# A fused chunk attention and leaky-ReLU layer pair: first layer in seven products for 15 of 18 blocks, sums kept in PSUM, uniform blocks, a new written-out order

## The chip, the core and the metric

The kernel runs on one core of a Trainium2 chip. TensorE multiplies 128x128 stationary tiles with moving tiles and writes PSUM; VectorE and ScalarE work in SBUF and PSUM; GpSimd works in SBUF and issues the loads; SyncE issues transposing DMAs and the stores. The engines run side by side and meet by semaphores. The metric is the device time of one execution in microseconds.

## The reference

q, k and v have 8 batches, 8 heads, 576 rows and 64 columns. Each 64-row chunk attends to itself; the result, as 4608 tokens of 512 columns, goes through two layers with a leaky ReLU between them.

```
scores = scale * np.matmul(q_c, k_c.transpose(0, 1, 2, 4, 3))      # chunks of 64 rows
scores = scores - np.max(scores, axis=-1, keepdims=True)
attn = np.exp(scores)
attn = attn / (np.sum(attn, axis=-1, keepdims=True) + 1e-09)
out = np.matmul(attn, v_c)
x = out.transpose(0, 2, 1, 3).reshape(B * S, H * D)               # 4608 x 512
h = x @ w_in                                                      # w_in 512 x 2048
g = np.maximum(0.01 * h, h)
return (g @ w_out).astype(np.float32)                             # w_out 2048 x 512
```

## The kernel before

*Attention* goes by 36 units of 128 tokens (two chunks of all heads). A unit u is loaded by `load_qk` (`g`, L91); its q and k are transposed by TensorE (`tq`, `tk`, tiles qp and kp, L512 and L517) or by SyncE's DMA (`tdq`, `tdk`, tiles QT and KT, L564 and L558) and copied to QZ and KT (`q`, `k`, `cq`). Then come scores (`s`, tile Sp, L584), maximum and difference (`m`, `b`, L593 and L598), exponential (`x`, tile ex, L604), its sum, a small addition and reciprocal (`z`, L610 to L614), the scaling (`n`, tile en, L620, on GpSimd from unit 10), a transpose (`e` and `c`, or `d` by DMA, L643), the product with v (`v`, tile xp, L656) and the copy to xT (`a`, L677), a ring of 1536 tokens.

*The layers* go by 19 blocks: two of 128 tokens and 17 of 256. The first layer of blocks 0 to 8 is plain: `mm1` (`A`, `M`, tile hT, L319), then `act1` (L333). Blocks 9 to 18 take it in seven half-size products in place of eight (Strassen's scheme in Winograd's form): token sums xs of x (`xs`, L387, mostly on GpSimd), weight sums WS (L365), products 1 to 7 (`wide`, `V`, L416) for both halves s of the hidden columns. Products 1, 6, 7 and 4 accumulate in one PSUM bank, xbank; after 1, 6 and 7 ScalarE copies the bank to SBUF (`lx`, tile xkeep, L447); products 2, 5 and 3 go to banks of their own (xpr) and VectorE adds them to the copies (`la`, L453); the leaky step reads copies or bank (`lp`, L435, a few on VectorE, L431).

*The second layer* is in seven products for all blocks of 256 tokens: token sums SG (`sum`, L203), weight sums TW (L174), `product` (`R`, L227: prX accumulates products 1, 6, 7 and 4; prW, prZ and pr take the others), `combine` (`comb`, L260 to L281). The two 128-token blocks use `mm2` (`B`, tile oP, L462).

Matmuls on a constant tile (`i`, tile idle, L686) fill TensorE's queue at the start. The order of all work is one hand-written list, ORDER: each word issues one step on its engine, and engines run their instructions in that order. BANKS names the PSUM bank of tiles that share four banks; qp, kp, ox and Sp have one each.

Of the kernel before, what the change touches and what calls it, by code (L numbers as in the profile page):

```python
# [16 lines left out]
def kernel(  # L17
# [36 lines left out]

# [3 lines left out]


# [47 lines left out]
    def load_w_in(f0, f1):
        for m in range(2):
            nc.gpsimd.dma_start(
                out=w_inT[m * CH:(m + 1) * CH, :, f0:f1],  # L110
                in_=moe_w_in[m * d_model // 2:(m + 1) * d_model // 2, f0:f1].rearrange("(t d) f -> d t f", d=D),
            )
# [45 lines left out]
    banks = iter(BANKS)

    def mm():  # L160
        return "m" + next(banks)

    TW: dict[int, bass.AP] = {}
    SG: dict[tuple[int, int], bass.AP] = {}
    bank: dict[tuple[int, str], bass.AP] = {}
    kept: dict[tuple[int, str], bass.AP] = {}
    opened: set[tuple[int, str]] = set()

    def weight_sum(n):
        b11, b12 = w_outT[:, :HF, :HM], w_outT[:, :HF, HM:]  # L170
        b21, b22 = w_outT[:, HF:, :HM], w_outT[:, HF:, HM:]
        x, y = {1: (b12, b11), 2: (b22, TW.get(1)), 3: (b22, b12), 4: (b21, TW.get(2))}[n]
        TW[n] = sbp.tile([128, HF, HM], FP16, name=f"TW{n}")
        nc.vector.tensor_tensor(out=TW[n], in0=x, in1=y, op=ALU.subtract)  # L174

    def rows(j):

        nh = BLOCKS[j] // 2
        halves_of = slice(0, nh), slice(nh, 2 * nh)
        return halves_of[::-1] if j in EARLY else halves_of  # L180

    def token_sums(j, n):
        if (j, n) in SG:
            return
        if j in EARLY:
            for a, p in {
                1: [(a, 1) for a in range(4)], 2: [(0, 2), (1, 2)], 3: [(0, 1), (1, 1), (0, 2), (1, 2)], 4: [(2, 2), (3, 2)],
            }[n]:
                need("act", j, a, p)
        if n in (2, 4):  # L190
            token_sums(j, n // 2)
        nh = BLOCKS[j] // 2
        one, two = rows(j)
        a11, a12 = gT[j][:, :HF, one], gT[j][:, HF:, one]
        a21, a22 = gT[j][:, :HF, two], gT[j][:, HF:, two]
        SG[j, n] = sbp.tile([128, HF, nh], FP16, name="SG", tag="gS", bufs=4, padded_shape=[128, HF, 128])
        x, y, op = {
            1: (a21, a22, ALU.add),
            2: (SG.get((j, 1)), a11, ALU.subtract),
            3: (a11, a21, ALU.subtract),  # L200
            4: (a12, SG.get((j, 2)), ALU.subtract),
        }[n]
        (nc.gpsimd if (j, n) in SG_POOL else nc.vector).tensor_tensor(out=SG[j, n], in0=x, in1=y, op=op)  # L203

    def product(j, n, i):
        one, two = rows(j)
        g, w = gT[j], w_outT
        where, left, right = {
            1: ("X", g[:, :HF, one], w[:, :HF, :HM]),
            2: ("W", g[:, HF:, one], w[:, HF:, :HM]),  # L210
            3: ("Z", SG.get((j, 4)), w[:, HF:, HM:]),
            4: ("X", g[:, HF:, two], TW.get(4)),
            5: ("Z", SG.get((j, 1)), TW.get(1)),
            6: ("X", SG.get((j, 2)), TW.get(2)),
            7: ("X", SG.get((j, 3)), TW.get(3)),
        }[n]
        if where != "X" and j in ONE:
            where = n
        if (j, where) not in bank:
            tag = None if j in EARLY else {"X": "qp", "Z": None if j in ZMM else "kp"}.get(where)  # L220
            bank[j, where] = psp.tile([128, 2, HM], FP32, name=f"pr{where}", tag=tag or mm(), bufs=1)
        to = bank[j, where]
        if j == LAST and n == 4:
            last_product(left, right)
            return
        for f in range(HF):
            nc.tensor.matmul(  # L227
                out=to[:, i, :],
                lhsT=left[:, f, i * 128:(i + 1) * 128],
                rhs=right[:, f, :],  # L230
                start=(j, where) not in opened,
# [641 lines left out]
```

## Time and profile before

Three runs: 274.97, 274.99 and 275.19 us. The profiled execution's span is 273.3 us; its own time stands in no record beside that span.

| engine | busy us | share of the span |
|---|---|---|
| TensorE | 265.9 | 97% |
| VectorE | 219.9 | 80% |
| ScalarE | 208.8 | 76% |
| GpSimd | 165.3 | 60% |

Busy time is the time in which at least one instruction of an engine runs. Matmuls overlap, so the duration of one is longer than the step from one to the next. The stretches of the profile give busy time, instructions and clock between two points of time; the chain follows what released each step back from the last instruction.

### The profile page before, as it was taken

To read this page: it belongs to the slowest core of one execution; us is meant where nothing else is said; L and a number is where in the kernel's file an instruction comes from. 1 tells how busy PE (TensorE), PEld (TensorE's weight loads), DVE (VectorE), ACT (ScalarE), POOL (GpSimd) and SP (SyncE) were. 2 spreads that over 40 slices of the span, in tenths; PEclk is the share of its full clock that TensorE was granted. 3 is DMA by queue.
4 is the path that set the end of the run, shared out by engine and by line. 5 is a ranking of instruction groups with operands and counts; after the bars stand their busy time and mean duration, and the time that the engine had idled before them with its cause. 6 is when DMAs were issued, how large, how long until landed. Compare 5 with 4: busy or idle time off the path is not lost.

```text
span 273.3 us, 9009 instructions
## 1 busy us (share of the span) xinstructions
PE 265.9 (97%) x3705; PEld 242.4 (89%) x3705; DVE 219.9 (80%) x427; ACT 208.8 (76%) x410; POOL 165.3 (60%) x190
## 2 busy tenths in 40 slices
PE   7889999999999999999999999999999999999994
PEld 3579958999999899998989999999999998999994
DVE  7786869999997668798677987977899879488783
ACT  6667635665779688666999989899999998857560
POOL 8848546783175448649689799689895636012100
PEclk9999999999999999999999999999999999999999
DMA  9999999999999999999999999799999503131113
GB/s 147 155 188 191 206 178 156 176 117 130 210 138 169 171 140 119 195 219 168 164 189 153 203 160 124 139 134 180 95 147 158 134 2 101 22 98 40 41 41 115
DMA packets 159241, 38.34 MB, mean 140 GB/s; under 512 B 150240, under 2 KB 154720, under 8 KB 159200
## 3 DMA queue, kind: packets, MB, share of 16 engines
q0 software_dynamic: 111392, 18.10, 98.3%
q1 hardware_dynamic: 46768, 19.41, 38.7%
q8 instruction: 29, 0.48, 0.7%
q10 hardware_dynamic: 1040, 0.26, 0.4%
q14 instruction: 12, 0.10, 0.2%
HBM read 36.70 MB, written 9.44 MB: 169 GB/s over the span
## 4 chain that ended last, share of the span: by engine, by line
PE 86%; DVE 5%; ACT 3%; POOL 3%; issue 2%; POOLq 0%; DVEq 0%; ACTq 0%
PE hT L319 20%; PE prX L227 20%; PE xbank L416 11%; PE xpr L416 9%; PE prZ L227 6%; PE pr L227 6%; PE prW L227 3%; PE Sp L584 3%; PE xp L656 3%; PE oP L462 3%; ACT QZ L539 1%; ACT gT L435 1%; PE kp L512 1%; PE qp L512 1%; POOL SG L203 1%
## 5 line engine op out<-in xcount | busy, mean ns | idle before, releaser
L319 PE MATMUL hT<-xT,w_inT 128*128 128x128 f16 (+1 forms) x768 | 62.4, 237 | 0.0
L319 PEld LDWEIGHTS <-w_inT 128*128 128x128 f16 x768 | 53.6, 98 | 2.8
L227 PEld LDWEIGHTS <-SG 128*128 128x128 f16 x544 | 51.0, 98 | 5.4
L620 POOL TENSOR_TENSOR en<-ex,zi 128x512 f16<-128x512 f16 x26 | 28.2, 1085 | 40.1 <-DVE zi L614 19.8
L453 DVE TENSOR_TENSOR xkeep<-xpr,xkeep 128x512 f32<-128x512 f32 x60 | 39.6, 681 | 13.7 <-ACT xkeep L447 9.6
L333 ACT ACTIVATE gT<-hT 128x512 f16<-128x512 f32 x64 | 36.6, 595 | 9.0 <-PE hT L319 8.9
L227 PEld LDWEIGHTS <-gT 128*128 128x128 f16 x400 | 37.3, 98 | 4.3 <-ACT gT L435 0.4
L447 ACT ACTIVATE xkeep<-xbank 128x512 f32<-128x512 f32 x60 | 34.6, 593 | 7.4 <-PE xbank L416 7.0
L416 PEld LDWEIGHTS <-WS 128*128 128x128 f16 x640 | 38.0, 98 | 0.5
L91 POOL DMA_DIRECT2D q_in<-in_q_dram x39 | 33.4, 861 | 7.0 <-DMA w_outT<-in_moe_w_out_dram 3.0
L91 POOL DMA_DIRECT2D k_in<-in_k_dram x39 | 32.6, 838 | 7.8 <-DMA VB<-in_v_dram 3.3
L227 PE MATMUL prX<-TW,SG 128*128 128x256 f16 x272 | 35.3, 273 | 0.0
L435 ACT ACTIVATE gT<-xkeep 128x512 f16<-128x512 f32 x56 | 33.4, 631 | 2.1 <-DVE xkeep L453 1.8
L260 ACT ACTIVATE keep<-prX 128x256 f32<-128x256 f32 x51 | 19.6, 384 | 16.9 <-PE prX L227 16.5
L416 PEld LDWEIGHTS <-w_inT 128*128 128x128 f16 x480 | 29.0, 98 | 0.9 <-issue 0.4
L203 DVE TENSOR_TENSOR SG<-gT 128x1024 f16<-128x1024 f16 x34 | 25.2, 740 | 4.7 <-ACT gT L333 2.9
L610 DVE TENSOR_REDUCE z<-ex 128x8 f32<-128x512 f16 x36 | 24.4, 679 | 4.9 <-ACT ex L604 4.7
L593 DVE TENSOR_REDUCE mx<-Sp 128x8 f32<-128x512 f32 x36 | 24.4, 677 | 4.5 <-PE Sp L584 4.5
L573 ACT ACTIVATE QZ<-QT 64x512 f16<-64x512 f16 x44 | 27.3, 627 | 0.9 <-PE Sp L584 0.3
L677 ACT ACTIVATE xT<-xp 128x512 f16<-128x512 f32 x36 | 21.5, 596 | 6.0 <-PE xp L656 5.8
L387 POOL TENSOR_TENSOR xs<-xT 128x256 f16<-128x256 f16 x18 | 12.5, 701 | 20.7 <-ACT xT L677 20.7
L98 POOL DMA_DIRECT2D VB<-in_v_dram x24 | 23.4, 987 | 0.0
(92 smaller groups left out, 486.0 us busy)
## 6 DMA issues: line engine op xcount, KB each, us to landing
out_dram<-osb SPq DMA_DIRECT2D x35, 256.0 KB, 4.1
q_in<-in_q_dram POOLq DMA_DIRECT2D x31, 128.0 KB, 5.9
k_in<-in_k_dram POOLq DMA_DIRECT2D x31, 128.0 KB, 6.7
VB<-in_v_dram POOLq DMA_DIRECT2D x8, 288.0 KB, 9.1
VB<-in_v_dram POOLq DMA_DIRECT2D x16, 144.0 KB, 5.3
w_inT<-in_moe_w_in_dram POOLq DMA_DIRECT2D x8, 256.0 KB, 7.2
w_outT<-in_moe_w_out_dram POOLq DMA_DIRECT2D x4, 512.0 KB, 11.6
q_in<-in_q_dram POOLq DMA_DIRECT2D x8, 64.0 KB, 6.3
```

What stands on the lines that cost most here:

```text
L91: nc.gpsimd.dma_start(out=to, in_=rows)
L203: (nc.gpsimd if (j, n) in SG_POOL else nc.vector).tensor_tensor(out=SG[j, n], in0=x, in1=y, op=op)
L227: nc.tensor.matmul(out=to[:, i, :], lhsT=left[:, f, i * 128:(i + 1) * 128], rhs=right[:, f, :], start=(j, where) not in opened, stop=(f == ...
L319: nc.tensor.matmul(out=hT[:, i, :], lhsT=w_inT[:, t, fc * 128:(fc + 1) * 128], rhs=xT[:, t, r0:r0 + tb], start=(t == 0), stop=(t == NT - 1),)
L333: nc.scalar.activation(out=gT[j][:, nf * a:nf * a + nf, c0:c0 + tb], in_=HT.pop((j, a, p)), func=AFT.Prelu, bias=0.0, scale=1.0, alpha=0.01,)
L416: nc.tensor.matmul(out=to[:, i, :], lhsT=left[:, t, i * 128:(i + 1) * 128], rhs=right[:, t], start=(n in (1, 2, 5) and t == 0 and i == 0), ...
L435: nc.scalar.activation(out=gT[j][:, f0:f0 + 4, hi * 128:hi * 128 + 128], in_=of, func=AFT.Prelu, bias=0.0, scale=1.0, alpha=0.01)
L447: nc.scalar.activation(out=XK[j, s, n], in_=XB[j, s], func=AFT.Copy, bias=0.0, scale=1.0)
L453: nc.vector.tensor_tensor(out=to, in0=of, in1=to, op=ALU.add)
L573: nc.scalar.activation(out=to, in_=QT[u][part], func=AFT.Copy, bias=0.0, scale=1.0)
L593: nc.vector.tensor_reduce(out=MX[u], in_=SP[u], axis=AXL.X, op=ALU.max)
L620: (nc.gpsimd if u >= UP else nc.vector).tensor_tensor(out=E[u], in0=ex, in1=ZI.pop(u).unsqueeze(2).to_broadcast((128, 8, CH)), op=ALU.mult)
```

## The change

Blocks are now 18 of 256 tokens. Blocks 0, 1 and 2 keep the plain first layer, in parts of 128 tokens; blocks 3 to 17 take it in seven products. All 18 take the second layer in seven. The wide sums are now made so: after product 1, the bank is copied to another bank (`ls`, tile seed) and product 2 accumulates on it; product 5 starts a bank xz, which is copied to SBUF (`lf`, tile x5); after product 6 VectorE adds xbank and x5 into xz (`la` with 3), where product 3 accumulates; after product 7 it adds xbank and x5 into x5 (`la` with 7). The leaky step reads seed, xz, xbank and x5. A mark ' on a word moves a step to the other engine: copies from ScalarE to VectorE, token sums and `n` from VectorE to GpSimd, z's small addition from VectorE to ScalarE. BANKS names the bank among eight for every PSUM tile and the slot of every SBUF tile. ORDER and the order of the loads are new throughout.

```diff
-    BLOCKS = 2 * [128] + 17 * [256]
-    EARLY = (2, 3, 4)
+    BLOCKS = 18 * [256]
+    LATE = (0, 1, 2)
+    FIVE = (0, 1, 2, 15, 16, 17)
+    HELD = 3
...
-        XK[j, s, n] = sbp.tile([128, 4, 128], FP32, name="xkeep", tag="xkeep", bufs=6)
-        nc.scalar.activation(out=XK[j, s, n], in_=XB[j, s], func=AFT.Copy, bias=0.0, scale=1.0)
...
-        nc.vector.tensor_tensor(out=to, in0=of, in1=to, op=ALU.add)
...
+    def wide_seed(j, s, other=0):
+        XW[j, s] = ps([128, 4, 128], "seed")
+        copy(other, XW[j, s], XB[j, s])
+
+    def wide_five(j, s, other=0):
+        X5[j, s] = sb([128, 4, 128], FP32, "x5", "xkeep", 6)
+        copy(other, X5[j, s], XZ[j, s])
+
+    def wide_add(j, s, n):
+        to = XZ[j, s] if n == 3 else X5[j, s]
+        nc.vector.tensor_tensor(out=to, in0=XB[j, s], in1=X5[j, s], op=ALU.add)
...
-        (nc.gpsimd if (j, n) in SG_POOL else nc.vector).tensor_tensor(out=SG[j, n], in0=x, in1=y, op=op)
+        (nc.gpsimd if other else nc.vector).tensor_tensor(out=SG[j, n], in0=x, in1=y, op=op)
...
-        "i33 y4 y2 I y0 y6 y1 tq0 q0.0 q0.1 w3 tk0 i5 k0 i6 s0 tq1 i4 m0 b0 q1.1.1 i13 tk1 q1.0.1 x0 k1 tq2 i8 s1 tk2 "
-        "z0 m1 b1 k2.1 n0 i6 q2.0.1 q2.1.1 x1 i9 i7 i13 e0 c0.1 z1 s2 tk3 v0 tq3 m2 n1 b2 a0 e1 c1 i7 v1 A0.0 x2 a1 "
+        "g2 y0 y1 i5.1 i73.0 y2 g1 I y4 If y3' i15.3 tq2 tk0 k0 tq0 tk2 q0.0 q0.1 tq1 s0 tk1 q1.1 q2.0' k2' q1.0 q2.1' s2 "
+        "m0 g3 tq3 k1 s1 tk3 b0 x0 q3.1 i25.4 m2 m1 b1 k3 q3.0 x1 s3 g6 tq6 b2 z0.0 z0.1 z1.0 x2 z0.2 q6.1 z2.0 tk6 i8.7 "
+        "g5 tk5 m3 L0 n0 z1.1 z1.2 tq5 q5.0 k6 i52.6 e0 i27.5 g4 z2.1' q6.0 tq4 y6' Q3 b3 x3 n1 e1 z2.2 z3.0 q5.1 n2 tk4 "
+        "z3.1 c0 z3.2 e2 Q1 k5 s5 v0 g8 q4.0' g7 Q0 c1 n3 e3 v1 k4 s6 a0 c2' v2 q4.1' s4 c3 v3 M0.3.1 a1' i2.2 m4 a2 "
```

On ScalarE, halfway through the program, copies of xbank to xkeep (L447) stood between the second layer's copies (keep, L260) and leaky steps (L435):

```order
L447 ACTIVATE xkeep<-xbank 128x512
L260 ACTIVATE keep<-prX 128x256
L447 ACTIVATE xkeep<-xbank 128x512
L435 ACTIVATE gT<-xkeep 128x4x128
L447 ACTIVATE xkeep<-xbank 128x512
L573 ACTIVATE QZ_67<-QT 64x8x64
```

The same place of the changed program, where a copy goes to a PSUM bank (seed, L200) or from xz to x:

```order
L384 ACTIVATE gT<-x_2868 128x4x128
L200 ACTIVATE seed<-xbank 128x512
L200 ACTIVATE keep<-prX 128x256
L384 ACTIVATE gT<-seed 128x4x128 x2
L200 ACTIVATE x_3238<-xz 128x512
L384 ACTIVATE gT<-xz 128x4x128
```

Leaky steps now read PSUM banks for three of four quarters, and of three copies two are left.

On VectorE, about half of its rows in, the sums of first-layer products (L453), combined outputs (osb, L281), token sums (SG, L203) and attention stood so:

```order
L203 TENSOR_TENSOR SG<-gT 128x1024
L453 TENSOR_TENSOR xkeep<-xpr,xkeep 128x512 x2
L281 TENSOR_TENSOR osb_3071<-prZ,keep 128x256
L593 TENSOR_REDUCE mx<-Sp 128x8
L453 TENSOR_TENSOR xkeep<-xpr,xkeep 128x512 x2
L281 TENSOR_TENSOR osb_2909<-prZ,keep 128x256
L203 TENSOR_TENSOR SG<-gT 128x1024
L203 TENSOR_TENSOR SG<-SG,gT 128x1024
L598 TENSOR_TENSOR Sp<-Sp,mx 128x512
```

In the changed program, at the same count of rows:

```order
L198 COPY QZ_66<-QT 64x8x64
L288 TENSOR_TENSOR Sp<-Sp,mx 128x512
L461 TENSOR_TENSOR x_2578<-xbank,x_2578 128x512
L502 TENSOR_TENSOR SG<-SG,gT 128x1024
L284 TENSOR_REDUCE mx<-Sp 128x8
L563 TENSOR_TENSOR ob<-prZ,keep 128x256
L502 TENSOR_TENSOR SG<-gT 128x1024
L198 COPY keep<-prX 128x256
L461 TENSOR_TENSOR xz<-xbank,x_2773 128x512
```

The copy of prX (keep) came from ScalarE, a sum is written to the bank xz, and the copy into QZ has come too; the small addition to z has gone to ScalarE in places.

On GpSimd, behind the first loads, all instructions were loads (q_in, k_in, VB of v, w_outT):

```order
L91 DMA k_in<-in_k_dram 128x8x64
L121 DMA w_outT<-in_moe_w_out_dram 128x4x512 x4
L91 DMA q_in<-in_q_dram 128x8x64
L91 DMA k_in<-in_k_dram 128x8x64
L98 DMA VB_64<-in_v_dram 64x36x64 x2
```

There the scaling of attention (en, L309) and a token sum (SG, L502) now stand between loads:

```order
L146 DMA w_outT<-in_moe_w_out_dram 128x4x512
L309 TENSOR_TENSOR en<-ex,z_829 128x512
L146 DMA w_outT<-in_moe_w_out_dram 128x4x512
L502 TENSOR_TENSOR SG<-gT 128x1024
L117 DMA q_in<-in_q_dram 128x8x64
```

Loads behind the token sum are issued after it.

More of the change, by code (lines that the diff above doesn't have):

```diff
@@ L158 @@
[L158 to L183, printed above, removed]
-            return
[L185 to L231, printed above, removed]
-                stop=(f == HF - 1),
-                skip_group_check=True,
-            )
-            opened.add((j, where))
@@ L497, with idle, copy @@
+    def idle(n, _=0):
+        t = ps([128, 512], "idle")
+        for i in range(0, n, 3):
+            c = 128 * min(3, n - i)
+            nc.tensor.matmul(out=t[:, :c], lhsT=warm[:, :128], rhs=warm[:, :c], start=True, stop=True)
+    def copy(other, to, of):
+        if other:
+            nc.vector.tensor_copy(out=to, in_=of)
+        else:
+            nc.scalar.activation(out=to, in_=of, func=AFT.Copy, bias=0.0, scale=1.0)
     QP: dict[int, bass.AP] = {}
@@ L651, in stage_v @@
[L651 to L652 removed]
+        XP[u] = ps([128, NT, 2, CH], "xp")
         for e in range(2):
@@ L666, in stage_v @@
-            if c == NCH - 1:
-                made.add(("batch", b))
-        XP[u] = xp
-    def load_v_piece(b, i):
-        made.add(("vl", b, i))
-        load_v_heads(b, i % 2, i // 2 * H // 4, i // 2 * H // 4 + H // 4)
-    def stage_a(u):
-        xp = XP.pop(u)
-        at = u * G % RING
-        nc.scalar.activation(out=xT[:, :, at:at + G], in_=xp, func=AFT.Copy, bias=0.0, scale=1.0)
-        assert state["tokens"] == u * G
-        state["tokens"] = (u + 1) * G
-    def idle(n):
-        t = psp.tile([128, 512], FP32, name="idle", tag=mm(), bufs=1)
-        for i in range(0, n, 3):
-            c = 128 * min(3, n - i)
-            nc.tensor.matmul(out=t[:, :c], lhsT=warm[:, :128], rhs=warm[:, :c], start=True, stop=True)
@@ L735, with stage_a, hidden, part_of @@
-    ORDER = (
[84 rows of a table removed]
+    def stage_a(u, other=0):
+        at = u * G % RING
+        copy(other, xT[:, :, at:at + G], XP[u])
+        groups.add(u)
+    gT: dict[int, bass.AP] = {}
+    HT: dict[tuple[int, int, int], bass.AP] = {}
+    def hidden(j):
+        if j not in gT:
+            gT[j] = sb([128, NFC, BLOCKS[j]], FP16, "gT", "gT", 3, padded_shape=[128, NFC, NB])
+        return gT[j]
+    def part_of(j, p):
+        return (128, (p - 1) * 128) if p else (BLOCKS[j], 0)
+    def mm1(j, a, p=0):
+        tb, c0 = part_of(j, p)
+        rows_ready(START[j] + c0, START[j] + c0 + tb)
+        r0 = (START[j] + c0) % RING
+        nf = 512 // tb
+        hT = ps([128, nf, tb], "hT")
+        for i in range(nf):
+            fc = nf * a + i
+            for t in range(NT):
+                nc.tensor.matmul(
+                    out=hT[:, i, :],
+                    lhsT=w_inT[:, t, fc * 128:(fc + 1) * 128],
+                    rhs=xT[:, t, r0:r0 + tb],
+                    start=(i == 0 and t == 0),
+                    stop=(t == NT - 1),
+                    skip_group_check=True,
+                )
+        HT[j, a, p] = hT
@@ new lines, in last_product @@
+    def last_product(left, right):
+        r0 = START[LAST] + halves_of(LAST)[1].start
+        for c in range(0, HM, HM // 2):
+            cut = slice(c, c + HM // 2)
+            of = ps([128, HM // 2], "prL")
+            for f in range(HF):
+                nc.tensor.matmul(out=of, lhsT=left[:, f, :], rhs=right[:, f, cut], start=(f == 0), stop=(f == HF - 1))
+            to = ob[LAST, 1][:, cut]
+            nc.vector.tensor_tensor(out=to, in0=of, in1=kept[LAST, 7][:, cut], op=ALU.add)
+            nc.sync.dma_start(out=out[r0:r0 + 128, cut], in_=to)
```

682 lines of the change are left out of this document (289 added, 393 removed), and 169 rows, old and new, of the table ORDER.

## The prediction, made before the changed kernel ran

> **What bounds the kernel now.** I read the page's shares first, then busy time by stretch.
>
> ```profile
> span 273.3 us, 9009 instructions
> PE 265.9 (97%) x3705; PEld 242.4 (89%) x3705; DVE 219.9 (80%) x427; ACT 208.8 (76%) x410; POOL 165.3 (60%) x190
> ...
> 0.00:20.00 20.00, 16.41 (x237) 11.16 (x238) 15.66 (x33) 12.96 (x19) 14.26 (x25) 1.00 1.62 162
> 20.00:60.00 40.00, 40.00 (x603) 35.48 (x601) 32.80 (x62) 24.93 (x50) 28.17 (x34) 1.00 1.98 172
> 60.00:100.00 40.00, 40.00 (x525) 37.06 (x524) 32.52 (x69) 28.66 (x57) 19.26 (x20) 1.00 1.89 161
> 140.00:180.00 40.00, 39.82 (x594) 37.74 (x592) 33.96 (x66) 37.10 (x75) 34.47 (x40) 1.00 1.53 152
> 180.00:220.00 40.00, 39.98 (x597) 37.85 (x595) 32.86 (x61) 38.09 (x79) 30.60 (x32) 1.00 1.27 140
> ```
>
> The columns of the stretches are PE, weight loads, VectorE, ScalarE, GpSimd, then granted clock (1.00 throughout) and DMA. From 20 us on TensorE misses 0.2 us in 160. The kernel is bound by the length of TensorE's queue. ScalarE at 95% (38.09 of 40) and VectorE at 85% (33.96) did not yet stall it. Next, the start in order of time (start us, us, engine, line, tiles, count, idle time before it and its releaser):
>
> ```profile
> 1.33 3.50 PE L686 MATMUL idle<-warm 128*128 128x384 f16 x11 [1.33 <-DVE zeros L137]
> 7.43 0.41 PE L584 MATMUL Sp<-KT,QZ 128*128 128x64 f16 x8 [0.72 <-DVE QZ L541]
> 11.59 2.07 PE L686 MATMUL idle<-warm 128*128 128x384 f16 x13
> 14.01 0.40 PE L628 MATMUL tpe<-ident,en 128*128 128x128 f16 x4 [0.35 <-DVE en L620]
> 17.44 1.95 PE L319 MATMUL hT<-xT,w_inT 128*128 128x128 f16 x32
> ```
>
> Until 17.44 us the queue holds attention of the first units, filler ("idle" products on a constant tile), and waits for VectorE and ScalarE. The first eleven fillers take 3.50 us, 0.32 each; thirteen later ones take 2.07, 0.16 each. So filler is real queue time: an idle product too many costs 0.16 us.
>
> A matmul's own duration is no price, since they overlap; the chain that ended last gives prices, for runs of equal matmuls:
>
> ```profile
> 22.68 3.58 PE hT L319 x64
> 34.53 1.73 PE oP L462 x8
> 124.39 1.75 PE hT L319 x16
> 154.79 0.89 PE xbank L416 x16
> 155.68 0.87 PE prX L227 x8
> 268.87 0.91 PE prL L244 x16
> ```
>
> That is 0.0556 us for 128 columns (0.89/16, 3.58/64), 0.109 for 256 (0.87/8, 1.75/16) and 0.216 for 512 (1.73/8). The chain's last matmul ends at 269.8; the end behind it (VectorE's sum, the last stores) is 3.5 us of the 273.3. The median of the runs, 274.99, stands 1.7 us above this span, and I carry the 1.7 over.
>
> **The change, part by part: TensorE.** *First layer.* Before: 512 plain matmuls of 128 columns, 256 of 256, 1120 of the seven-product kind: 28.5 + 27.9 + 62.3 = 118.7 us. Now 384 plain ones and 15 blocks of 112, 1680: 2064 x 0.0556 = 114.8. Gain **3.9 us**.
>
> *Second layer.* Before: 944 of 256 columns and 32 of 512 (the two 128-row blocks): 102.9 + 6.9. Now 1000 of 256: 109.0. The 16 halves of the last product stay. Gain **0.8**.
>
> *Transposes.* Units 11 to 13 go through SyncE's DMA in place of TensorE: 24 fewer, **1.3**. They add six transposing DMAs; SyncE's queue, 90 instructions long, has no compute behind it.
>
> *Filler.* 41 idle products become 72; those of 384 columns grow from 34 to 66. 32 x 0.16 = **5.1 us more**. Useful work shrinks by 6.0, the queue by only **0.9**. So the result hangs on waits.
>
> **Waits at the start.** In the table of stretches' manner, TensorE is idle 3.6 us of the first 20 (16.41 busy; 1.3 before anything is there); counting from matmul start to matmul start and taking off the prices above, the waits there cost 4.5 us beside the 1.3 and the slow first fillers, since each wait also drains the pipeline. Now seven units' scores stand before the first layer's first matmul. Walking the order: tq2, tk0, tq0, tk2, tq1 run from 7.9 to 10.3 us; s0 needs both halves of QZ, two ScalarE copies behind k0, about 10.9: a wait of 0.55. s1 and s3 wait 0.5 each for k1 and q3.0, v3 0.2 for c3. That is 1.8, and about 1.2 for changes of kind where a weight load isn't hidden: 3.0 against 4.5. Gain **1.5**. Bounds: all 4.5 saved, or, if the walk errs by a step or two of 0.7 us on ScalarE, 1 lost. The first plain matmul then starts near 24.5 us, not 17.4. Its weights (the last quarter of w_in, now loaded behind six units and a batch of v) come by GpSimd's queue; two issues in order of time, and the page's row on issues with its median from issue to landing:
>
> ```profile
> 16.31 0.62 POOL L109 DMA_DIRECT2D w_inT<-in_moe_w_in_dram  x1 [0.61 <-DMA w_inT<-in_moe_w_in_dram]
> 17.59 0.61 POOL L109 DMA_DIRECT2D w_inT<-in_moe_w_in_dram  x1 [0.65 <-DMA w_inT<-in_moe_w_in_dram]
> ...
> k_in<-in_k_dram POOLq DMA_DIRECT2D x31, 128.0 KB, 6.7
> ```
>
> Each half quarter (0.5 MB read) follows the last by 1.3 us; GpSimd waits for a landing before it issues another, so the loads run at the DMAs' pace. The first unit lands 6.7 us after its issue at 1.25, near 8; five more units of 0.5 MB, the batch of 1.2 MB and two half quarters at 1.3 us for 0.5 MB are 12.2 more: near 20, an estimate from these rows, and 22.5 if the units' shorter rows go at three quarters of that rate. Hidden, with 2 us of cover at the worse end. Were loads 3 us later than that, first layer and end would move by 1.
>
> **VectorE, ScalarE and GpSimd.** Prices of what moves, from the groups of instructions (count | busy us, mean ns of one | idle time before):
>
> ```profile
> L612 DVE TENSOR_TENSOR ze<-z,tiny 128x8 f32<-128x8 f32 x36 | 6.6, 182 | 1.2
> L453 DVE TENSOR_TENSOR xkeep<-xpr,xkeep 128x512 f32<-128x512 f32 x60 | 39.6, 681 | 13.7 <-ACT xkeep L447 9.6 <-PE xpr L416 3.9
> L203 DVE TENSOR_TENSOR SG<-gT 128x1024 f16<-128x1024 f16 x34 | 25.2, 740 | 4.7 <-ACT gT L333 2.9 <-ACT gT L435 1.8
> L281 DVE TENSOR_TENSOR osb<-prZ,keep 128x256 f32<-128x256 f32 x22 | 9.3, 421 | 4.6 <-PE prZ L227 3.1 <-ACT keep L260 1.2
> L541 DVE COPY QZ<-qp 64x512 f16<-64x512 f16 x19 | 7.9, 417 | 1.8 <-ACT QZ L539 1.5 <-PE qp L512 0.2
> L387 DVE TENSOR_TENSOR xs<-xT 128x256 f16<-128x256 f16 x2 | 0.6, 282 | 0.0
> L447 ACT ACTIVATE xkeep<-xbank 128x512 f32<-128x512 f32 x60 | 34.6, 593 | 7.4 <-PE xbank L416 7.0 <-DMA out_dram<-osb 0.2
> L203 POOL TENSOR_TENSOR SG<-gT,SG 128x1024 f16<-128x1024 f16 x8 | 17.4, 2173 | 9.3 <-DVE SG L203 4.0 <-ACT keep L260 2.7 <-ACT xkeep L447 2.6
> L620 POOL TENSOR_TENSOR en<-ex,zi 128x512 f16<-128x512 f16 x26 | 28.2, 1085 | 40.1 <-DVE zi L614 19.8 <-ACT xkeep L447 9.8 <-ACT gT L435 3.0
> ```
>
> A seven-product half now needs two copies and two sums of 512 columns, before three and three; with 30 halves for 20 the sums stay 60. VectorE loses 13 token sums (-9.6 us), 13 copies into QZ (-5.4) and 17 small sums of z (-3.1, at 0.182); it gets 17 copies of 256 columns (+7.1), 14 of 512 and 7 of xT (+14.3), 9 from QT (+3.8, at the nearest row; at least +1.8 by half of it), 17 token sums of x (+4.8), and leaky steps, en and the rest (+4). Sum: +16 of durations, +11 if each overlaps the next as L453 does (busy 39.6 for 60 x 681 = 40.9, and its follower starts earlier still): 219.9 becomes **231 to 236 us**. ScalarE loses 14 copies of 512 (-8.3), 13 of 256, 7 of xT: to below 200. GpSimd gets 17 token sums x 2.17 = +36.9: about 201. Neither is full. Copies from a bank to another bank (seed) aren't in the trace; nearest is L447, 0.593, and nothing says by which sign it differs: 0.4 to 0.8 on 30 ScalarE and VectorE copies, off the path unless those engines bind.
>
> VectorE is nearer to it: summed along the order by these prices (0.60 where rows follow each other), 178 us of its work stand before block 11's first second-layer product, R11.1, and 188 of TensorE's. It can't begin scores before s0, 11.2 us, with 4.6 done: 185 of 188. I take no stall beyond the 0.3 that the stretches show, since ScalarE at 95% cost no more.
>
> Sum: 274.99 - 0.9 (queue) - 1.5 (start) = **272.6 us**.
>
> **Rivals.** *VectorE loses turns to GpSimd (slower).* Two meetings in order of time, the group of GpSimd's xs, and token sums by tile (least/median/greatest ns):
>
> ```profile
> 76.52 1.32 POOL L620 TENSOR_TENSOR en<-ex,zi 128x512 f16<-128x512 f16 x1 [3.68 <-DVE zi L614]
> 76.86 1.53 DVE L203 TENSOR_TENSOR SG<-gT,SG 128x1024 f16<-128x1024 f16 x1
> 204.40 1.98 DVE L203 TENSOR_TENSOR SG<-gT 128x1024 f16<-128x1024 f16 x1
> 204.76 1.06 POOL L620 TENSOR_TENSOR en<-ex,zi 128x512 f16<-128x512 f16 x1
> ...
> L387 POOL TENSOR_TENSOR xs<-xT 128x256 f16<-128x256 f16 x18 | 12.5, 701 | 20.7 <-ACT xT L677 20.7
> ...
> L203 DVE TENSOR_TENSOR SG<-gT x34: 640/684/1979, 30.3 to 265.7; 128x1024 f16<-128x1024 f16 x34
> L203 DVE TENSOR_TENSOR SG<-gT,SG x9: 640/687/1532, 42.1 to 265.1; 128x1024 f16<-128x1024 f16 x9
> ```
>
> A token sum that lies over a tensor operation of GpSimd ends only after it: 1.53 and 1.98 us where the median is 0.69 (least, median and greatest stand in the last rows). Summed over VectorE's rows, nine operations stand so far over the median of their kind, by 5.1 us together, 0.56 each, and TensorE did not feel it. GpSimd's tensor operations grow from 71 us (28.2 en, 17.4 SG, 36 of xs at 0.7) to 106 (23, 25 and 39 of them), VectorE's two-input operations in SBUF from 77 to 97: at the old rate of meetings 9 x 1.5 x 1.26 = 17. At 0.56 us that is 9.6 us; at 0.85, since a SG lasts 2.17 for en's 1.09, 14; I take 12. VectorE at R11.1 is then at 185 + 12 = 197 against TensorE's 188 + 3 of waits: 6 late, less about 2 by which its work is ordered ahead. Time 272.6 + 4 = **276.6**, and 278.5 with the 14. It decides once VectorE loses over 8 us before R11.1 (191 + 2 - 185). For it: so little slack. Against: a changed order may keep the two apart.
>
> The Trainium skill, GPSIMD Engine Reference, section Key points, has GpSimd share its SBUF interfaces with VectorE, with contention for instructions that have two SBUF inputs. It speaks against moving token sums to GpSimd: by it both engines pay at each meeting, and by the sum without it neither does. The rows above agree with it (1.98 us for 0.69); it is this rival, and 30% is what the bare order lets me give it.
>
> *The filler fits exactly (faster).* All early waits go, 4.5 in place of 1.5, and the 0.3 later: 272.6 - 3.3 = **269.3**. Against: copies on ScalarE stand in line before s0.
>
> *No difference.* The start costs what it did plus 0.7 us of new waits in the middle, where eight shared banks now order TensorE behind VectorE: **274.9**. The other way of no effect, that the work isn't saved, is excluded: the products are counted in the program.
>
> **How the numbers follow.** About 0.2% (0.55 us) can be told from no change. Forecast (270.5 to 274.4) 45%; exact filler (below 270.5) 16%; no difference (274.4 to 275.5) 9%; VectorE bound (above) 30%. Faster 0.61, same 0.09, slower 0.30. The range runs from 268.8 to 278.5: each end leaves a tenth out. For the cases that are faster alone it is 268.8 to 274.4.
>
> **What would show it.** The first plain matmul at 23 to 26 us, with 72 idle products before it. TensorE without idle time from there: 40.00 in the stretches. If VectorE binds, those fall to 38 or less between 40 and 190 us with "DVE" as the releaser, VectorE's own share is over 95%, and token sums longer than 1 us are more than nine. If ScalarE binds, seeds and copies of xz would release TensorE. Wrong altogether would be a start that waits for w_in (a DMA as the releaser of the first plain matmuls), or a longer end than 3.5 us.

## The result, and the profile after

The changed kernel takes **303.61 us** in the median of four runs (299.31 to 307.57), the kernel before 275.09 beside it (274.97 to 276.08). The ratio is 1.09, with a 95% interval of 1.0825 to 1.0975. Two of the four runs lie more than 1.5% above the fastest; such runs, the profiled one among them (305.35, its granted clock of 0.983 as in the two others), are left out of the ratio and of the medians and differences below, so that the changed kernel counts there as 300.59, or 25.5 more than before. The forecast was 272.6, and its range ended at 278.5.

First the page's span and shares, then busy time by stretch in the columns that the prediction used (TensorE, weight loads, VectorE, ScalarE, GpSimd, granted clock, DMA):

```profile
span 303.6 us, 9463 instructions
PE 273.4 (90%) x3912; PEld 249.9 (82%) x3912; DVE 251.4 (83%) x458; ACT 196.2 (65%) x391; POOL 201.9 (67%) x207
```

```profile
0.00:20.00 20.00, 16.86 (x212) 11.06 (x213) 13.40 (x29) 12.64 (x21) 16.90 (x28) 1.00 1.85 155
20.00:60.00 40.00, 36.20 (x626) 33.65 (x625) 35.85 (x67) 29.17 (x56) 25.44 (x29) 1.00 1.75 169
60.00:100.00 40.00, 37.41 (x512) 34.81 (x512) 37.46 (x75) 28.25 (x60) 29.46 (x32) 0.96 2.19 146
100.00:140.00 40.00, 33.93 (x492) 31.33 (x490) 34.40 (x59) 27.68 (x57) 29.01 (x31) 0.96 1.80 151
140.00:180.00 40.00, 35.70 (x549) 33.48 (x547) 38.67 (x67) 29.75 (x62) 31.16 (x36) 1.00 1.92 151
180.00:220.00 40.00, 36.59 (x527) 33.99 (x524) 34.57 (x65) 30.75 (x65) 28.02 (x27) 1.00 1.09 141
```

TensorE was full from 20 us on before. Now it misses 3 to 6 us of every 40, and in two stretches its granted clock is 0.96. VectorE is at 94% in one stretch (37.46) and 97% in another (38.67), yet at 86% (34.40) where TensorE loses most. So no single engine is full where the loss is greatest. TensorE's longest waits, by releaser (total us, times, longest):

```profile
PE xbank L442 <- DVE xz L461: 6.1, 3, 3.8
PE prZ L525 <- DVE ob L563: 3.4, 2, 2.4
PE Sp L277 <- DMA KT<-k_in: 3.2, 1, 3.2
PE xp L335 <- DMA et<-en: 3.1, 5, 2.0
PE xz L442 <- ACT ex L294: 2.4, 1, 2.4
PE hT L370 <- DVE sh L288: 1.4, 1, 1.4
```

VectorE, transposing DMAs and ScalarE all release late. Counted from matmul start to matmul start, with the prediction's prices taken off, what TensorE loses grew from 6.9 us to **38.3** in the profiled run. The prices themselves, summed over the instructions of the two traces, are 261.30 us before and 260.65 after. Of the 31.4 us more, waits make 27.1 and half-rate matmuls 4.3. This is a stretch with both, in order of time, and then the row of the half-rate part in the columns above:

```profile
223.37 0.40 PE L335 MATMUL xp<-et,VB 128*128 128x64 f16 x8
227.53 1.01 PE L442 MATMUL xbank<-xs,WS 128*128 128x128 f16 x8 [3.76 <-DVE xz L461]
228.33 1.91 PE L525 MATMUL prZ<-TW,SG 128*128 128x256 f16 x8
230.04 1.27 PE L525 MATMUL prX<-TW,SG 128*128 128x256 f16 x8
...
227.11:230.52 3.41, 2.99 (x19) 2.33 (x19) 1.39 (x4) 0.00 (x0) 0.00 (x0) 0.50 0.39 77
```

Eight products of 256 columns take 230.04 - 228.33 = 1.71 us, 0.214 each in place of 0.109, at a granted clock of 0.50. There are three such stretches of 3.41 us, from 83.75, 128.12 and 227.11 us on. Each begins at or near the end of a wait, of 2.5, 3.3 and 3.9 us; they lost 1.6, 1.3 and 1.4 us. The Trainium skill (TensorE: Matmul & The Clock Gate, Part 1) tells of a return to half rate after an idle window of about 3.4 us. The trace agrees for the longest wait, but 3.3 and 2.5 us sufficed too, and a wait of 2.6 us at 157.2 was not followed by it. The three starts lie 13 and 29 times 3.413 us apart, so the clock seems to be set anew at such points: the wait of 2.6 us lay across one of them (158.84), the other three between two of them for all but a few tenths of a us.

Where does VectorE's lateness come from? One place in order of time, and the spread by tile (least, median, greatest ns):

```profile
168.42 0.74 POOL L418 TENSOR_TENSOR xs<-xT 128x256 f16<-128x256 f16 x1
168.83 2.73 DVE L198 COPY QZ<-QT 64x512 f16<-64x512 f16 x1
169.06 1.11 POOL L309 TENSOR_TENSOR en<-ex,z 128x512 f16<-128x512 f16 x1
170.06 0.72 POOL L418 TENSOR_TENSOR xs<-xs,xT 128x256 f16<-128x256 f16 x1
170.68 0.72 POOL L418 TENSOR_TENSOR xs<-xT 128x256 f16<-128x256 f16 x1
...
171.48 0.67 DVE L198 COPY x<-xz 128x512 f32<-128x512 f32 x1
```

```profile
L502 DVE TENSOR_TENSOR SG<-gT x23: 640/683/2476, 46.1 to 293.6; 128x1024 f16<-128x1024 f16 x23
...
L198 DVE COPY QZ<-QT x9: 291/580/2729, 74.4 to 203.8; 64x512 f16<-64x512 f16 x9
```

A copy of 0.29 us ends only behind a whole train of GpSimd's operations. Each kind of VectorE's rows has a floor, its 15th percentile. Summed over the rows that stand more than 0.1 us above it, the time above the floor grew from 5.5 to **31.7 us**; I call this VectorE's loss. The second suspect stands in the view of DMAs (median us from issue to landing), where QT was at 5.1, KT at 5.2 and et at 5.2 before:

```profile
et<-en SPq DMA_TRANSPOSE x30, 4.5
QT<-q_in SPq DMA_TRANSPOSE x25, 6.7
KT<-k_in SPq DMA_TRANSPOSE x25, 6.1
```

### The profile page after: what moved, and what is told of

Same layout as the page of the kernel before. It is cut to its first block, busy times and chain, and to the rows that moved or that the text cites. A ratio compares the mean times of both kernels' runs of the same rounds, so it can differ in the third digit from the quotient of the medians.

```text
span 303.6 us, 9463 instructions
## 1 busy us (share of the span) xinstructions
PE 273.4 (90%) x3912; PEld 249.9 (82%) x3912; DVE 251.4 (83%) x458; ACT 196.2 (65%) x391; POOL 201.9 (67%) x207
## 4 chain that ended last, share of the span: by engine, by line
PE 55%; DVE 20%; DMA 12%; ACT 7%; issue 4%; DVEq 0%; ACTq 0%
PE prX L525 13%; PE xbank L442 11%; PE prZ L525 8%; DMA QT<-q_in 6%; PE xz L442 5%; PE prW L525 4%; PE idle L194 4%; DMA et<-en 4%; PE seed L442 3%; DMA KT<-k_in 3%; DVE QZ L198 3%; ACT QZ L200 2%; DVE SG L502 2%; DVE WS L404 2%; ACT gT L384 2%
## 5 line engine op out<-in xcount | busy, mean ns | idle before, releaser
L442 PEld LDWEIGHTS <-WS 128*128 128x128 f16 x960 | 59.5, 99 | 10.9 <-issue 9.2
L309 POOL TENSOR_TENSOR en<-ex,z 128x512 f16<-128x512 f16 x23 | 24.4, 1059 | 26.2 <-DVE z L305 17.9
L442 PE MATMUL xbank<-xs,WS 128*128 128x128 f16 x480 | 36.0, 220 | 6.3 <-DVE xz L461 6.1
L502 POOL TENSOR_TENSOR SG<-gT 128x1024 f16<-128x1024 f16 x13 | 28.4, 2188 | 17.0 <-ACT gT L384 10.1
L502 POOL TENSOR_TENSOR SG<-gT,SG 128x1024 f16<-128x1024 f16 x9 | 20.3, 2253 | 17.6 <-DVE SG L502 8.8
L200 ACT ACTIVATE keep<-prX 128x256 f32<-128x256 f32 x40 | 15.2, 381 | 23.0 <-PE prX L525 23.0
L200 ACT ACTIVATE QZ<-QT 64x512 f16<-64x512 f16 x41 | 25.4, 625 | 3.7 <-DMA QT<-q_in 2.3
L370 PE MATMUL hT<-xT,w_inT 128*128 128x128 f16 x384 | 24.0, 219 | 3.0 <-DVE sh L288 1.4
L200 ACT ACTIVATE xT<-xp 128x512 f16<-128x512 f32 x29 | 17.1, 595 | 14.2 <-PE xp L335 14.1
L384 ACT ACTIVATE gT<-xbank 128x512 f16<-128x512 f32 x30 | 17.7, 595 | 11.7 <-PE xbank L442 11.6
L461 DVE TENSOR_TENSOR xz<-xbank,x 128x512 f32<-128x512 f32 x30 | 20.7, 692 | 5.4 <-ACT x L200 2.6
L461 DVE TENSOR_TENSOR x<-xbank,x 128x512 f32<-128x512 f32 x30 | 20.3, 681 | 5.0 <-PE xbank L442 4.9
L384 ACT ACTIVATE gT<-xz 128x512 f16<-128x512 f32 x30 | 17.8, 594 | 8.5 <-PE xz L442 8.3
```

The source lines that it names most:

```text
L200: nc.scalar.activation(out=to, in_=of, func=AFT.Copy, bias=0.0, scale=1.0)
L309: (nc.gpsimd if other else nc.vector).tensor_tensor(out=EN[u], in0=EX[u], in1=Z[u, 2].unsqueeze(2).to_broadcast((128, 8, CH)), op=ALU.mult)
L370: nc.tensor.matmul(out=hT[:, i, :], lhsT=w_inT[:, t, fc * 128:(fc + 1) * 128], rhs=xT[:, t, r0:r0 + tb], start=(i == 0 and t == 0), stop=( ...
L384: nc.scalar.activation(out=to, in_=of, func=AFT.Prelu, bias=0.0, scale=1.0, alpha=0.01)
L442: nc.tensor.matmul(out=to[:, i, :], lhsT=left[:, t, i * 128:(i + 1) * 128], rhs=right[:, t], start=(n in (1, 5) and t == 0 and i == 0), st ...
L461: nc.vector.tensor_tensor(out=to, in0=XB[j, s], in1=X5[j, s], op=ALU.add)
```

## The experiments

Four theories are tested: **Sharing** (GpSimd's tensor operations stretch VectorE's), **Load** (VectorE has too much work of its own), **Late transposes**, and, after the first four runs, **In step** (several late sources, each hidden behind another). The kernel before measured 275.0 to 275.8 beside them all. Times are medians; *loss* is VectorE's, as above.

### Moving work between engines

First, the nine copies from QT to QZ go to ScalarE, by taking the mark ' off nine words of ORDER.

```diff
- ... cq14.0' ... cq15.1' ...
+ ... cq14.0 ... cq15.1 ...
```

> The changed kernel with the nine copies of QT into QZ that VectorE makes given to ScalarE; else the same order. Sharing (VectorE stands still while GpSimd runs a train of tensor operations): these nine were 0.29 us at their shortest and 2.73 at their longest, and lost 7.7 us together; without them TensorE waits 5 to 9 us less: 291 to 297 against about 300 to 304. Load (VectorE has too much work, sharing or not): 9 x 0.29 = 2.6 us less work, at most 2.6 us faster: 298 to 301. Late transposes (DMA transposes land after 6 to 9 us where they took 5): no change, 299 to 304.

Measured: 301.46 us. The loss fell from 31.7 to 16.4, but the time did not fall. In its profile TensorE waits for other things:

```profile
PE xp L335 <- DMA et<-en: 6.4, 5, 4.1
PE xp L335 <- DMA VB<-in_v_dram: 3.3, 1, 3.3
PE hT L370 <- DVE sh L288: 2.7, 1, 2.7
```

Next, all 25 token sums of GpSimd go back to VectorE.

```diff
- sum0.1' ... sum17.3'
+ sum0.1 ... sum17.3
```

> The changed kernel with all 25 token sums of GpSimd given back to VectorE; else the same order. Sharing: GpSimd's tensor time falls from 109 to about 58 us and VectorE's losses from 31 to 10 to 15, while its work grows by 25 x 0.62 = 15.5: net 2 to 6 us better, 294 to 300. Load: VectorE has 15 us more on an engine that is the bound: 310 to 318. Late transposes: no change but for the load on VectorE, 300 to 305.

Measured: 298.81 us. The loss was 10.2 us, and TensorE's longest wait was for KT (5.7 us in two). This is far from Load's 310 or more; between Sharing's 294 to 300 and Late transposes' 300 to 305 it doesn't decide.

Then no tensor operation is left on GpSimd: en, xs and sum words lose their mark, 87 in all.

```diff
- n4' ... xs3.1' ... sum0.1' ...
+ n4 ... xs3.1 ... sum0.1 ...
```

> The changed kernel with no tensor operation on GpSimd at all (token sums, sums of x and the scaling of attention all on VectorE). Sharing: nothing is lost, no VectorE operation of a kind is over 1.1 times its shortest; VectorE's work is 223 + 15.5 + 14 + 10 = 262 us and is the bound: 278 to 290, faster than the changed kernel though VectorE does 39 us more. Load: 39 us more on the bound: 325 to 345. Late transposes: no better than 300.

Measured: 308.71 us, with a loss of 1.0. VectorE had taken on work (255.5 us busy), and TensorE waited up to 5.3 us for et. That contradicts Load's 325 or more as well as Sharing's 290 or less; Late transposes alone allowed it.

Then 59 copies and 8 leaky steps lose their mark and go from VectorE to ScalarE.

```diff
- q2.0' ... k2' ... c2' ... a1' ... comb1.6' ... lp16.0.5'
+ q2.0 ... k2 ... c2 ... a1 ... comb1.6 ... lp16.0.5
```

> The changed kernel with every copy and leaky step of VectorE (57 of them: 14 of prX, 8 seeds, 6 x5, 7 xT, QZ, KT, et, 8 leaky steps) given to ScalarE, whose work grows from 196 to about 222 us. VectorE loses 27 us of work, GpSimd keeps its 25 token sums. Sharing: the losses of the copies (8 to 10 of 31 us) go, the other 20 stay, and the freed VectorE hides a part: 283 to 292. Load: VectorE is at 196 us and no bound any more: 272 to 278. Late transposes: 298 to 303.

Measured: 308.53 us, though VectorE was down to 205.0 us busy. That is far from Load's 272 to 278, and none of the three had it so late. But these four runs moved work onto another engine as they took it away, so they can't tell a cause without weight from one whose relief was paid for elsewhere.

### Leaving work out

The next kernels shorten instructions and move nothing. Buffers are kept as fixed tiles, whose first use is whole.

```diff
-(nc.gpsimd if other else nc.vector).tensor_tensor(out=SG[j, n], in0=x, in1=y, op=op)
+c = cols(SG[j, n], 128, 16, other)
+(nc.gpsimd if other else nc.vector).tensor_tensor(out=SG[j, n][:, :, :c], in0=x[:, :, :c], in1=y[:, :, :c], op=op)
```

(`cols` gives 16 of 128 columns where GpSimd makes the sum and the buffer was filled before; xs alike; en with 8 of its 64 columns a head.)

> The changed kernel, but GpSimd's tensor operations (token sums, xs, en; 87 of them, 109 us) run on an eighth of their columns, apart from the first use of each buffer. The rest of those outputs is left out, nothing is moved to another engine, no order changes. Unlike the runs that moved work, this takes the sharing away without a price elsewhere. Sharing alone (VectorE's 31.7 us of lost time is the cause): VectorE's loss under 5 us and the time falls by 20 us or more, to 275 to 284. Load alone (VectorE's own work is too close to TensorE's): at most 5 us less, 297 to 302. Late transposes alone: the loss of VectorE falls, the waits for et, KT and QT stay, 295 to 302. In step (several late sources, each hidden behind another, so that taking one away brings out the next): 287 to 295.

Measured: 295.30 us, with a loss of 5.7. This easing alone is worth 5.3 us, much less than Sharing needs, and just short of what I had set for In step; Late transposes' 295 to 302 has it too. It also makes GpSimd's results earlier, so it bounds the sharing from above as long as the loads are whole. TensorE's longest waits are now for transposing DMAs:

```profile
PE Sp L290 <- DMA KT<-k_in: 5.7, 2, 3.3
PE xp L349 <- DMA et<-en: 4.5, 5, 1.5
```

Next, VectorE's 60 sums of the first layer are shortened:

```diff
-nc.vector.tensor_tensor(out=to, in0=XB[j, s], in1=X5[j, s], op=ALU.add)
+nc.vector.tensor_tensor(out=to[:, :, :16], in0=XB[j, s][:, :, :16], in1=X5[j, s][:, :, :16], op=ALU.add)
```

> The changed kernel, but VectorE's 60 sums of 512 columns in the first layer run on an eighth of their columns (the rest of the result is left out): VectorE loses about 30 us of its own work, and nothing else gets it. GpSimd's work stays. Load alone: 272 to 282. Sharing alone: the lost turns stay but fall on an engine with 30 us of room, 297 to 303 if a lost turn costs where it happens, less if room absorbs it. Late transposes alone: 298 to 304. In step: 288 to 297.

Measured: 296.33 us in one run and 301.43 to 302.46 in the other three. Some 30 us less work on VectorE (220.7 us busy) gave no gain that these runs resolve. Both edits together:

> Both edits: GpSimd's tensor operations and VectorE's 60 first-layer sums on an eighth of their columns. What is left of the time above TensorE's own queue (262) then comes from neither VectorE's load nor the sharing. Sharing or Load: 270 to 276. Late transposes: 290 to 300, with the waits of TensorE at xp, Sp and QZ. In step: 276 to 286, with waits for DMA transposes (et, KT, QT) as the largest that remain.

Measured: 296.55 us. VectorE was at 200.7 us busy (68%), its loss at 5.2, and still 21 us were missing. TensorE's longest waits were now for KT (up to 4.5 us). This is the range of Late transposes; In step had been set too low by 10 us here. So the transposes were put earlier, each as soon as its buffer and its input allow:

```diff
-... g11 G0.2.2 ... W3.1 tdq11 R1.1 ... z9.2 tdk11 R1.2
+... g11 tdk11 tdq11 G0.2.2 ... W3.1 R1.1 ... z9.2 R1.2
```

> The changed kernel, but every transposing DMA (50 of QT and KT, 30 of et) stands in the order as early as its buffer and its input allow, 6 to 140 steps sooner; nothing else moves. Late transposes alone: TensorE's and VectorE's waits for et, KT and QT (some 10 us, and what follows from them) go, and the time falls to 285 to 293. Sharing alone, or Load alone: 299 to 305. In step: 295 to 302, since SyncE then waits in line for each input and VectorE's late copies stay.

Measured: 341.32 us. Transposes landed sooner (QT 4.3, KT 4.7), yet the kernel lost 41 us more. SyncE takes its instructions in line, and a transpose that waits for its input or buffer holds up those behind it; one wait for en was 39.7 us long there.

Next the loads bring in less, which shortens what the transposes share the DMA engines with:

```diff
+if some:
+    to, rows = to[:, :2], rows[:, :2]
...
+h1 = h1 if b < NVB else h0 + 1
```

(q and k bring two heads of eight once their buffer was filled before, which is what `some` says; v brings one head from the third batch on.)

> The changed kernel, but loads bring in less: two heads of eight for q and k once each buffer has been filled, one head for v from the third batch on (the rest of these inputs is left out). The DMA engines get about a third of the loads' bytes from some 70 us on, and GpSimd's issues get shorter; order and computing instructions stay. Late transposes (now read as: SyncE's transposes wait for loads to land and share the DMA engines with them): the median from issue to landing of QT and KT falls from 6 to 7 us to about 3, TensorE's waits for et, KT, QT go, 288 to 295. Sharing alone: at most the part of it that lies over GpSimd's issues, 299 to 304. Load alone: 300 to 305. In step: 290 to 298.

Measured: 292.42 us, ratio 1.0642 (1.0582 to 1.0701). This is the largest effect of one edit, 8.2 us. In the view of DMAs (QT bears its fixed tile's name q_in) QT and KT land in half the time:

```profile
et<-en SPq DMA_TRANSPOSE x30, 3.5
q_in<-q_in SPq DMA_TRANSPOSE x25, 3.3
KT<-k_in SPq DMA_TRANSPOSE x25, 3.2
```

VectorE's loss was still 25.2, and what TensorE waits for longest is VectorE:

```profile
PE prZ L536 <- DVE ob L574: 3.4, 2, 2.4
PE xbank L453 <- DVE xz L472: 2.5, 2, 1.4
```

Now all three edits:

> All three at once: GpSimd's tensor operations on an eighth, VectorE's 60 first-layer sums on an eighth, lighter loads. With the first two alone the time was 296.6, so neither VectorE's work nor the sharing is left; the rest is 20 us over the kernel before. Late transposes and loads: 272 to 282, the granted clock back to 0.99 or more, and no wait of TensorE over 2.5 us. If the time stays above 288, the loads and transposes aren't what is left either, and it is the order itself with its named buffers (each engine waits for the others' last readers).

Measured: **278.75 us**, ratio 1.0127 (1.0108 to 1.0145). The stretches again:

```profile
20.00:60.00 40.00, 36.87 (x636) 34.31 (x635) 35.44 (x69) 29.50 (x58) 23.39 (x29) 1.00 1.78 166
60.00:100.00 40.00, 39.95 (x574) 37.70 (x572) 34.83 (x85) 30.85 (x65) 25.45 (x39) 1.00 0.93 106
100.00:140.00 40.00, 39.15 (x601) 37.02 (x599) 30.05 (x72) 34.92 (x71) 19.78 (x37) 1.00 1.18 139
140.00:180.00 40.00, 40.00 (x628) 38.19 (x626) 32.87 (x75) 32.88 (x70) 19.10 (x35) 1.00 1.25 130
180.00:220.00 40.00, 39.93 (x570) 37.64 (x569) 24.55 (x64) 30.76 (x64) 9.81 (x26) 1.00 0.50 102
```

From 60 us on TensorE is all but full, at full clock. The next run eases GpSimd's operations and the loads, but leaves VectorE's sums whole, and so tells whether VectorE's own work matters:

> GpSimd's tensor operations on an eighth and lighter loads, with VectorE's own work whole (left out: most of these sums and of the inputs). Load counts only if this stays well above the run with all three (278.75): Load 285 to 291. Sharing and loads alone make the loss: 278 to 281.

Measured: 278.29 us, the same. **VectorE's own load is not a cause** once the other two are eased. GpSimd's operations alone are worth 5.3 us, the loads alone 8.2, and both 22.3: some 9 us hang on both. This also rules out Late transposes alone, by which GpSimd's operations would be worth nothing once the loads are light; they are worth 14.1 there (292.42 to 278.29). So the loss has two sources, Sharing (with GpSimd's late results) and late loads and transposes, and each hides behind the other, as TensorE's waits in the two single runs show. That is In step with VectorE's load struck out; its numbers for single edits were too hopeful.

### Parts of the change on the kernel before

Seventeen token sums of the kernel before move to GpSimd:

```diff
-SG_POOL = ((8, 4), (9, 4), (10, 4), (11, 4), (12, 4), (13, 4), (14, 4), (15, 4))
+SG_POOL = (the same) + tuple((j, 3) for j in range(5, 16)) + tuple((j, 1) for j in range(10, 16))
```

> The kernel before, with 17 more of its token sums on GpSimd (the change has 17 more there), nothing else. VectorE loses 17 x 0.69 = 12 us of work, GpSimd gets 17 x 2.17 = 37. Sharing: VectorE's loss over each kind's least duration rises from 5.5 to 12 us or more, and the time with it, by 1 to 6 us (276 to 281), if there is no slack; with slack the loss shows and the time stays at 275. Load: 273 to 275.5. Late transposes: 275 to 276.

Measured: 292.86 us, 17.8 more and far beyond Sharing's 6. The loss rose to 16.1, and there is more in the waits:

```profile
DVE SG L203 <- POOL SG L203: 14.6, 5, 4.6
PEld L227 <- POOL SG L203: 6.1, 6, 1.5
PE prX L227 <- POOL SG L203: 5.0, 5, 1.3
```

Sum 2 on VectorE waits for sum 1 on GpSimd, and TensorE waits for its operands. A sum that takes 2.17 us in place of 0.69 and stands in a queue with the loads is late itself, besides slowing VectorE.

Units 11 to 13 of the kernel before go through SyncE's DMA:

```diff
-... tk11 ... k11 ... tq11 Q11
+... tdk11 ... tdq11 cq11.0 cq11.1
```

> The kernel before, with units 11 to 13 transposed by SyncE's DMA as in the change, in place of 24 transposes of TensorE (1.3 us of its queue), nothing else. Late transposes: waits for QT and KT of these units by TensorE or VectorE, 276 to 281. Sharing and Load: 273.5 to 275.5, the work saved and no more.

Measured: 284.81 us, 9.8 more. GpSimd's part of the timeline:

```profile
60.99 1.18 POOL L98 DMA_DIRECT2D VB<-in_v_dram  x1
74.77 0.90 POOL L91 DMA_DIRECT2D q_in<-in_q_dram  x1 [12.60 <-DMA QT<-q_in]
75.65 0.90 POOL L91 DMA_DIRECT2D k_in<-in_k_dram  x1
76.55 1.07 POOL L620 TENSOR_TENSOR en<-ex,zi 128x512 f16<-128x512 f16 x1
```

A load must wait until the transpose has read its buffer, and en stands behind that load in GpSimd's queue. QT of unit 11 had no lead here, so the run was repeated with lead for QT and with earlier loads:

```diff
-... g10 comb2.7 ... x8 G3.3.2 ... g11 ... tdk11 ... tdq11 cq11.0 cq11.1
+... g10 g11 comb2.7 ... x8 tdq11 G3.3.2 ... tdk11 tdq12 ... cq11.0 cq11.1
```

> The kernel before with units 11 to 13 transposed by DMA, each QT at least 35 steps and each KT at least 34 ahead of its reader (in the first such run QT of unit 11 stood right ahead of it), and the loads of units 11 and 12 earlier. If lead was all that was missing: 273.5 to 276. If transposing DMAs in that stretch cost by themselves, through GpSimd's loads that wait for them: 278 to 285.

Measured: 284.43 us, the same. TensorE's longest wait is the end of that chain (load, en, et, xp):

```profile
POOL q_in L91 <- DMA QT<-q_in: 19.9, 3, 7.5
...
PE xp L656 <- DMA et<-en: 6.4, 1, 6.4
```

The two parts on the old order cost 17.8 and 9.8 us. That their sum is near the change's 25.5 shows nothing by itself, since the new order is another.

### Lead, a control, and the filler

In the changed kernel the transposes of QT and KT go 12 steps earlier, in their own order (here unit 11's):

```diff
-... V3.0.1 d8 s10 v7 a7 xs3.1' xs3.2' W2.0 W3.0 sum1.2 W4.0 W2.1 W3.1 tdq11 R1.1
+... V3.0.1 tdq11 d8 s10 v7 a7 xs3.1' xs3.2' W2.0 W3.0 sum1.2 tdk11 W4.0 W2.1 W3.1 R1.1
```

> The changed kernel with the 50 transposing DMAs of QT and KT 12 steps earlier in the order (about 3 us), in the same order among themselves and not ahead of the last reader of their buffer; all work and all loads as they were. If their lateness is the matter and lead cures it: 292 to 299. If they only wait in SyncE's line for loads and buffers: 300 to 308. Sharing alone or Load alone: 300 to 305.

Measured: 313.84 to 323.76 us in four runs. With 25 steps:

> The same with 25 steps (about 6 us). If lead cures: 288 to 297, less than with 12 steps. If SyncE's line is the matter: 303 to 320, more than with 12 steps, toward the 341 of the run in which they stood as early as they could.

Measured: 326.11 us. Here QT lands in 4.4 and KT in 4.9, but TensorE's longest wait is another:

```profile
PE xp L335 <- DMA et<-en: 20.8, 5, 6.1
```

The earlier transposes hold up et in SyncE's line. Lead cures nothing in this order; it only moves the wait to et.

A control takes GpSimd's narrow operations and the lighter loads to the kernel before, with fixed buffers for SG, xs, en and the inputs:

> The kernel before with GpSimd's tensor operations on an eighth of their columns and the lighter loads (the rest of these sums and inputs is left out), as a control. If sharing and late loads are what the change ran into and the kernel before did not: 272 to 275.5, since its TensorE misses 0.2 us in 160. If they cost the kernel before as well, and the change only showed it: 262 to 271.

Measured: 281.86 us, slower. The reason is one wait:

```profile
135.86 0.61 PE L447 MATMUL xbank<-xs,WS 128*128 128x128 f16 x8
140.56 0.61 PE L617 MATMUL Sp<-KT,QZ 128*128 128x64 f16 x8 [4.09 <-ACT QZ L606]
```

The control makes that wait itself: its fixed buffers put the transpose of unit 26 into the buffer of unit 22 ahead of the copy of unit 22. Up to there TensorE had lost as much as in the kernel before (6.0 us against 6.1 by the count above). So the easing gave the kernel before nothing in that half; for the rest the control is spoilt.

Last, the eased changed kernel loses seven of the eight `i` words of its start (70 idle products; the expectation miscounted them as 68):

> The changed kernel with all three easings (278.75), and without the idle products at the start except the first: 68 products, some 12 us of TensorE's queue in the first 25 us, are gone. If they only fill waits: the time stays, 277 to 281. If some of the 3 us over the kernel before are filler that waits for nothing: 273 to 277. If the granted clock falls without them: over 281.

Measured: 278.60 us, the same. What TensorE loses grew by 11.1 us (11.5 to 22.6), about what the filler had taken. Part of it is the clock, for without the filler the products of the start ran at half rate up to 25.6 us:

```profile
15.98 1.06 PE L246 MATMUL kp<-ident,k_in 128*128 128x128 f16 x8
16.84 0.63 PE L246 MATMUL qp<-ident,q_in 128*128 128x128 f16 x4
```

Eight products take 0.86 us, 0.107 each in place of 0.056. (The run's mean clock of 1.00 doesn't show this: the clock's records begin only at 25.6 us there.) Yet the first plain matmul came only 0.5 us later (25.93 for 25.43), and the end no later. The filler keeps the clock up at the start and fills waits; it costs and gains nothing here.

No version that was run beats the kernel before.

## Why the prediction was wrong, point by point

- **TensorE's queue: right.** Forecast 0.9 us shorter, measured 261.30 - 260.65 = 0.65. But the 5.1 us of new filler in that sum was no cost, as the last run shows for the eased kernel: it and the waits are one term.
- **The start: nearly right.** The first plain matmul came at 25.27 us (forecast 24.5). Up to 26 us TensorE lost 5.1 us, in the kernel before 6.0: a gain of 0.9, not 1.5. Unforeseen were 3.5 us of waits in the plain first layer up to 50 us, where before there were none; the longest was released by VectorE's sh. The products that waited read nothing that sh makes; they take over the PSUM bank that it reads. The rival of no effect had such waits in shared banks, but at 0.7. They stay in the eased kernels (3.2 us of 11.5) and are most of why those end 3 us over the kernel before.
- **The failed step is the pricing of transposes and stalls.** The prediction took the stalls at almost nothing, and TensorE lost 31.4 us more. It said that SyncE's queue "has no compute behind it" and "I take no stall beyond the 0.3 that the stretches show". The kernel before with three transposed units lost 9.8 us, and its chain shows what stands behind SyncE: the loads that need the buffer, and en behind those loads. In the changed kernel with lighter loads, QT's transposes landed in 3.3 us instead of 6.7, and the time fell by 8.2.
- **The rival of lost turns had the right mechanism, but its price was too small.** It set 12 us of loss, at most 14, and 276.6. The trace has 31.7 - 5.5 = 26 us more. The old rate of 0.56 to 0.85 us a meeting missed that a VectorE operation waits out a train of GpSimd's. Its sign, more than nine token sums over 1 us, didn't come: there were five, and the loss lay in copies too (7.7 us in the nine from QT). Still, this easing alone is worth 5.3 us, near the 4 that the rival gave it. It needed the late loads and transposes for the two to grow to 22.
- **VectorE's 178 us against 188 was no bound.** With 30 us less of VectorE's sums the time did not fall by anything that the runs resolve, and by nothing once the other two sources were eased. The work itself was priced a little high: 251.4 us busy less the 26 of added loss is 225, where 231 to 236 was forecast. ScalarE and GpSimd came out as forecast (196.2 and 201.9 us busy).
- **A term that was missing:** the granted clock falls after long waits. It cost 4.3 us.
- **A slip in the rivals:** the terms of "no difference" give 274.99 - 0.9 + 0.7 = 274.8, not 274.9. It changes nothing.

What stays open: the single worths of 5.3 and 8.2 us rest on two to four runs each and are sure to some 3 us only. Open too is whether the lighter loads help by shorter landings alone. They also shortened GpSimd's issues (99.1 to 87.4 us in all) and VectorE's loss (31.7 to 25.2). And why a particular wait is late was followed in two chains only, not in all.

## What to carry to other kernels

Where the busiest engine has almost no idle time, the slack of every other queue must be read before work is put on it: for each moved DMA, who waits for the buffer it reads, and what stands behind that waiter. To find causes in such a kernel, shorten suspected instructions without moving them, singly and together, since a cause that hides behind another shows only when both are gone. Price work moved to GpSimd by how late its result is (2.17 us for 0.69 here) and by whole trains of its operations, not by single meetings.

## What the runs showed of the hardware beyond that

- A 64x512 f16 copy of VectorE inside SBUF took from 0.29 to 2.73 us. It started beside a GpSimd operation that had three more behind it without a gap, and it ended behind the last. The Trainium skill (SBUF — State Buffer, section on the two separate sides) tells of a lock that holds the shared ports for the whole instruction. Here the copy didn't come in between two instructions of the train either.
- The median time from issue to landing of QT's transposing DMA was 6.7 us with full loads and 3.3 with about a quarter of q's and k's. The loads beside it are not all: with full loads it was 5.1 in the kernel before, and 4.3 where all transposes stood early (at 341.32 us).
- Without 70 of 72 idle products the matmuls of the start ran at half rate up to 25.6 us, with them only up to some 5 us; the time was the same.
- In every trace with more than one stretch of half rate, the stretches start whole multiples of 3.413 us apart (14, 19, 23, 31 and more where all transposes stood early). Up to the last product they last one to four times that long.
